# Transposes of a transformer block on the DMA crossbar instead of TensorE

## The chip, the cores and the metric

The kernel runs on one core of one Trainium2 chip. The metric is the device time of one execution in microseconds; lower is better. Before the change it is 750.04 us, the median of three runs (748.21 to 750.16).

## The reference

One layer on 2048 rows of width 1024, in bf16: a layernorm without scale or shift, sliding-window attention (32 heads of 32 columns, window of 256 rows, causal), a residual sum, a second layernorm, and a feed-forward part with SiLU (inner width 3584) and its own residual.

```python
def _layernorm(x, axis=-1, eps=1e-5):
    m = jnp.mean(x, axis=axis, keepdims=True)
    v = jnp.var(x, axis=axis, keepdims=True)
    return (x - m) / jnp.sqrt(v + eps)

def _A_ref(x, wqkv, wo):          # H = 32, Dh = 32, W = 256
    q, k, v = ...                 # x @ wqkv, split into heads
    scores = jnp.einsum("bhqd,bhkd->bhqk", q, k) * (Dh ** -0.5)
    mask = (idx[:, None] - idx[None, :] >= 0) & (idx[:, None] - idx[None, :] < W)
    p = _softmax(jnp.where(mask[None, None], scores, -1e9), axis=-1)
    return (p @ v, heads joined) @ wo

h  = x + _A_ref(_layernorm(x), A_wqkv, A_wo)
h2 = h + silu(_layernorm(h) @ B_w1) @ B_w2
```

(The attention function is abridged here: the split and joining of heads are written in words.)

## The kernel before

The 2048 rows are cut into four blocks of 512 rows (b = 0 to 3), each of four tiles of 128 rows (j = 0 to 3). TensorE multiplies along the partition axis, so whatever a product contracts over must lie on the 128 partitions. Three activations are produced with their rows on the partitions and are therefore transposed before use:

- the normalized input, tile by tile, into lnT_b (the helper ln_transpose, lines 173 to 176): eight 128x128 transposes on TensorE into the PSUM tile tp_ps, then one copy of 128x1024 out of it;
- the normalized attention result, by the same helper, into ln2T;
- the attention output of one group of four heads, from a ring of three SBUF tiles obuf into qT (attn_transpose, lines 281 to 285): four transposes into tp_ps, then one copy of 128x512. The result takes the place of the queries of that head group, which are no longer needed.

There is one tp_ps for all of them. The copies are VectorE's, but for block 0 of the first layernorm, whose copies are ScalarE's.

The program is written out in the order in which each engine is to work; there is no scheduler. Every engine and every DMA queue takes its instructions in that order and waits, instruction by instruction, for the data and the buffers that it needs. All transfers are issued on SP's queue.

The stages, in order:

1. Weights and the first rows are loaded. Block 0 is normalized and transposed tile by tile and its value projections follow (lines 293 to 300). Then come block 0's query and key projections in eight head groups (from line 327); with them, two steps after each group, run the statistics, normalization and transposes of block 1, as a list of small functions (ln1_steps).
2. Three attention loops, b = 1, 2, 3 (line 336 on). Loop b has 24 steps: 8 head groups of three score pieces, called A, B and C. In each step TensorE computes the scores of one piece for block b-1 into two PSUM tiles sc (a pair of heads in each), then one of the 24 projection products of block b (8 matmuls of 128x512), then one pending piece of the previous head group's end: attention output for the first pair of heads, for the second pair, and in the third step the transpose of that output. ScalarE takes the exponentials of the scores (two of them, one for each sc tile, line 242), GpSimd masks them. Loops 1 and 2 also carry the first layernorm of block b+1: its statistics and normalization from step 1 on, its four transposes at steps 11, 14, 17 and 20, each behind the attention transpose of that step. The loads of the next block's rows are issued at the head of a loop.
3. A last attention loop of 24 steps for block 3's scores. In place of the projections stand the output projections (wo_group) of blocks 0 to 2, each with a residual load, a sum on VectorE and, after every second, a store to h_dram. From step 9 on it carries the second layernorm of block 0 (ln2_steps): a load from h_dram, statistics, normalization, and the four transposes at steps 19 to 22. The feed-forward weights are loaded on the way.
4. Four feed-forward blocks (line 395 on). The first product of a block is 28 groups of 8 matmuls (h1_group, line 406), each followed by a tanh on ScalarE and a multiplication on VectorE. The end of the last head group (its attention transpose too) stands behind the first three groups of block 0, and block 3's output projections from group 6 on. The second product is 8 groups of 28 matmuls (line 448), two for each tile j; behind each group VectorE adds the residual (line 450) and SP stores 128 KB of the output (line 452). Two steps of the next block's second layernorm follow each group: load and first statistics behind group 1, and so on, the four transposes behind groups 6 and 7, two behind each.

The first product of a block needs all four transposed tiles before its first matmul, since one matmul takes 512 columns, those of the whole block. The same holds for the query and key products; a value product needs one tile alone.

Of the kernel before, what the change touches and what calls it, by code (L numbers as in the profile page):

```python
# [14 lines left out]
P = 128  # L15
# [21 lines left out]
def kernel(  # L37
# [10 lines left out]
    nc = tc.nc  # L48
# [36 lines left out]
    tp_ps = ps.tile([P, 1024], BF16, name="tp_ps")  # L85
    acc_ps = [ps.tile([P, 512], F32, name=f"acc{i}") for i in range(2)]

    def view(region, off, *dims):
        n = 1
        for d in dims:  # L90
            n *= d
        ap = region[:, off:off + n]
        if len(dims) == 2:
            return ap.rearrange("p (a b) -> p a b", b=dims[1])
        if len(dims) == 3:
            return ap.rearrange("p (a b c) -> p a b c", b=dims[1], c=dims[2])
        return ap
# [3 lines left out]
    lnT_b = [view(r_w, 24576, KT, 512), view(r_t, 0, KT, 512)]  # L101
# [4 lines left out]
    qT = [view(r_a, (4096, 8192, 12288, 0)[b], G, 512) for b in range(NB)]  # L106
# [7 lines left out]
    obuf = [view(r_n, 512 * i, 4, P) for i in range(3)]  # L114
    h_blk = [view(r_a, w2_off + 4096 * 4, 4, D)] + [view(r_e, 8192, 4, D)] * 3
    ln2T = [view(r_a, w2_off + 4096 * 5, KT, 512), view(r_e, 0, KT, 512), view(r_e, 4096, KT, 512), view(r_e, 0, KT, 512)]
# [22 lines left out]
    ident = const.tile([P, P], BF16, name="ident")  # L139
# [10 lines left out]
    def ln_stats(xt, st, j):  # L150
        stats = small.tile([P, 2, 6], F32, name="ln_st", tag="ln_st")
        for c in range(2):
            nc.vector.bn_stats(out=stats[:, c, :], in_=xt[:, c * 512:(c + 1) * 512])  # L153
        nc.vector.bn_aggr(out=st[:, j, :], in_=stats[:])

    def ln_rstd(st, rs, lo, hi):
        n = hi - lo
        var = small.tile([P, 4], F32, name="ln_var", tag="ln_var")
        t = small.tile([P, 4], F32, name="ln_t", tag="ln_t")
        va, ta, y = var[:, 0:n], t[:, 0:n], rs[:, lo:hi]  # L160
        nc.vector.tensor_scalar(out=va, in0=st[:, lo:hi, 1], scalar1=LN_EPS, scalar2=None, op0=ALU.add)
        nc.vector.tensor_scalar(out=y.bitcast(I32), in0=va.bitcast(I32), scalar1=1, scalar2=None, op0=ALU.logical_shift_right)
        nc.vector.tensor_scalar(out=y.bitcast(I32), in0=y.bitcast(I32), scalar1=-1, scalar2=0x5F3759DF, op0=ALU.mult, op1=ALU.add)
        for _ in range(3):
            nc.vector.scalar_tensor_tensor(out=ta, in0=y, scalar=-0.5, in1=va, op0=ALU.mult, op1=ALU.mult)
            nc.vector.tensor_tensor(out=ta, in0=ta, in1=y, op=ALU.mult)
            nc.vector.scalar_tensor_tensor(out=y, in0=ta, scalar=1.5, in1=y, op0=ALU.add, op1=ALU.mult)

    def ln_norm(xt, st, rs, j):
        nc.vector.tensor_scalar(out=xt, in0=xt, scalar1=st[:, j, 0:1], scalar2=rs[:, j:j + 1],  # L170
                                op0=ALU.subtract, op1=ALU.mult)

    def ln_transpose(xt, dst, j, copy):
        for kt in range(KT):
            nc.tensor.transpose(out=tp_ps[:, kt * P:(kt + 1) * P], in_=xt[:, kt * P:(kt + 1) * P], identity=ident[:])  # L175
        copy(out=dst[:, :, j * P:(j + 1) * P], in_=tp_ps[:].rearrange("p (k q) -> p k q", q=P))  # L176

    def ln_tiles(tag):
        st = small.tile([P, 4, 2], F32, name=f"st_{tag}", tag=f"st_{tag}")
        rs = small.tile([P, 4], F32, name=f"rs_{tag}", tag=f"rs_{tag}")  # L180
        return st, rs
# [98 lines left out]

    def attn_transpose(b, g):
        i = b * G + g
        for qt in range(4):
            nc.tensor.transpose(out=tp_ps[:, qt * P:(qt + 1) * P], in_=obuf[i % 3][:, qt, :], identity=ident[:])
        nc.vector.tensor_copy(out=qT[b][:, g, :], in_=tp_ps[:, 0:512])

    def tail_of(b, g):
        return [lambda: attn_out(b, g, 0), lambda: attn_out(b, g, 1), lambda: attn_transpose(b, g)]

    dve, act = nc.vector.tensor_copy, nc.scalar.copy  # L290
# [3 lines left out]
    for j in range(4):  # L294
        ln_stats(x_ring[j], st, j)
        ln_rstd(st, rs, j, j + 1)
        ln_norm(x_ring[j], st, rs, j)
        ln_transpose(x_ring[j], lnT_b[0], j, act)
        v_group(0, j, 0, act)
        v_group(0, j, 1, act)  # L300
# [3 lines left out]
    def ln1_steps(b):  # L304
        st, rs = ln_tiles("a")
        xs = [x_ring[(b % 2) * 4 + j] for j in range(4)]
        steps = [lambda j=j: ln_stats(xs[j], st, j) for j in range(4)]
        steps.append(lambda: ln_rstd(st, rs, 0, 4))
        for j in range(4):
            steps.append(lambda j=j: ln_norm(xs[j], st, rs, j))  # L310
        return steps, [lambda j=j: ln_transpose(xs[j], lnT_b[b % 2], j, dve) for j in range(4)]

    def ln2_steps(b):
        st, rs = ln_tiles("b")
        hb = h_blk[b]
        load = lambda: nc.sync.dma_start(out=hb, in_=h_dram[b * 512:(b + 1) * 512, :].rearrange("(j p) d -> p j d", p=P))
        steps = [load]
        steps += [lambda j=j: ln_stats(hb[:, j, :], st, j) for j in range(4)]
        steps.append(lambda: ln_rstd(st, rs, 0, 4))
        for j in range(4):  # L320
            steps.append(lambda j=j: ln_norm(hb[:, j, :], st, rs, j))
        for j in range(4):
            steps.append(lambda j=j: ln_transpose(hb[:, j, :], ln2T[b], j, dve))
        return steps

    steps = sum(ln1_steps(1), [])
    for g in range(G):
        qk_group(0, 0, g, act)
# [7 lines left out]
    for b in range(1, NB):  # L336
        dense = [lambda j=j, c=c: v_group(b, j, c, dve) for j in range(4) for c in range(2)]
        dense += [lambda w=w, g=g: qk_group(b, w, g, dve) for g in range(G) for w in range(2)]
        if b + 1 < NB:
            for j in range(4):  # L340
                load_x(b + 1, j)
            steps, turns = ln1_steps(b + 1)
        else:
            steps, turns = [], []
            nc.sync.dma_start(out=wo[:, 0:4, :], in_=wo_v[:, 0:4, :])
            nc.sync.dma_start(out=wo[:, 4:8, :], in_=wo_v[:, 4:8, :])
        n = 0
        for g in range(G):
            for kind in KINDS:
                scores(b - 1, g, kind)  # L350
                dense[n]()
                if pending:
                    pending.pop(0)()
                if steps and n >= 1 and n != 3:
                    steps.pop(0)()
                elif turns and n % 3 == 2:
                    turns.pop(0)()
                n += 1
            pending = tail_of(b - 1, g)
        assert not steps and not turns  # L360
# [8 lines left out]
    steps = []  # L369
    n = 0  # L370
    for g in range(G):
        for kind in KINDS:
            scores(NB - 1, g, kind)
            b, j, c = dense[n]
            if c == 0:
                nb, nj = (b, j + 1) if j < 3 else (b + 1, 0)
                if nb < NB - 1:
                    load_res(nb, nj, x2d)
            wo_group(b, j, c)
            if pending:  # L380
                pending.pop(0)()
            if n % 2 == 0 and n // 2 < KT:
                nc.sync.dma_start(out=w1[:, n // 2, :], in_=w1_v[:, n // 2, :])
            if n == 9:
                steps = ln2_steps(0)
            if n == 17:
                nc.sync.dma_start(out=w2[0], in_=w2_v[:, 0:4, :])
            if steps and n >= 9:
                steps.pop(0)()
            n += 1  # L390
        pending = tail_of(NB - 1, g)
# [28 lines left out]
    for b in range(NB):  # L420
# [4 lines left out]
        for ft in range(FT):  # L425
# [7 lines left out]
            if b == 0 and 6 <= ft < 14:  # L433
                j, c = divmod(ft - 6, 2)
# [4 lines left out]
        if b == 0:  # L439
            load_w2(6)  # L440
        steps = ln2_steps(b + 1) if b + 1 < NB else []
        for j in range(4):
            if j < 3:
                load_res(b, j + 1, h_dram)
            for c in range(2):
                acc = next_acc()
                for ft in range(FT):
# [5 lines left out]
                                  in_=t_out[j % 2][:, c * 512:(c + 1) * 512])  # L453
# [35 lines left out]
```

## Time and profile before

| | us |
|---|---|
| median of three runs | 750.04 |
| the profiled execution | 748.3 |
| its span, first to last instruction | 746.6 |
| TensorE matmuls busy | 708.6 |
| VectorE busy | 322.7 |
| ScalarE busy | 257.1 |
| copies out of tp_ps of 128x512, 32 on VectorE | 13.3 |

A profile is of one execution. Its span leaves out what lies before the first and behind the last instruction (1.7 us here). A row of the timeline gives the start in microseconds from the start of the span, the length, the engine (PE is TensorE's matmuls, PEld its weight loads, DVE VectorE, ACT ScalarE, POOL GpSimd, SPq the issuing of transfers on SP's queue), the line of the kernel, the operation, output and input, their shape, the count of instructions merged into the row, and in brackets how long the engine was idle before it and what ended that. Matmuls are pipelined: a row of several is shorter than their number times the length of one.

The DMA rows give a queue's packets, megabytes and the time that the packets took as a share of 16 engines; the rows of issues give the size of a transfer and the median time from issue to landing.

### The profile page before, as it was taken

How to read it: one execution, taken by the hardware profiler on the slowest of the kernel's cores; microseconds unless marked ns; L12 is line 12 of the kernel's file. 1: busy time of each engine (PE TensorE's matmuls, PEld its weight loads, DVE VectorE, ACT ScalarE, POOL GpSimd, SP SyncE). 2: the span in 40 equal slices, each digit the busy share in tenths (PEclk: the TensorE clock that was granted, in tenths of full speed). 3: DMA queues.
4: the chain of work that ended last, by engine and by line, in shares of the span. 5: the costliest groups of instructions: out<-in, count | busy, mean ns of one | idle time of the engine just before them, and what ended most of it. 6: DMA issues, size and time to landing. Idle time of an engine off the chain costs nothing.

```text
span 746.6 us, 12719 instructions
## 1 busy us (share of the span) xinstructions
PE 708.6 (95%) x5266; PEld 351.5 (47%) x5358; DVE 322.7 (43%) x705; ACT 257.1 (34%) x325; POOL 172.2 (23%) x375
## 2 busy tenths in 40 slices
PE   6899989988999999899999989999899999999997
PEld 3444545555555554454444444444444444444443
DVE  7356744854444445754343423325224343244111
ACT  2315555766777776642230003310023300133000
POOL 1004545665666766630000000000000000000000
PEclk9999999999999999999999999999999999999999
DMA  9510001000100177636204110012010021100010
GB/s 312 195 43 15 1 3 57 2 2 2 58 2 2 52 260 290 212 136 240 71 1 155 36 35 16 0 40 74 21 36 1 0 93 36 43 0 1 17 47 22
DMA packets 28138, 49.06 MB, mean 66 GB/s; under 512 B 1968, under 2 KB 12208, under 8 KB 28080
## 3 DMA queue, kind: packets, MB, share of 16 engines
q1 hardware_dynamic: 28080, 48.24, 19.1%
q8 instruction: 42, 0.69, 0.4%
q14 instruction: 16, 0.13, 0.1%
HBM read 39.85 MB, written 8.39 MB: 65 GB/s over the span
## 4 chain that ended last, share of the span: by engine, by line
PE 90%; DVE 5%; DMA 2%; issue 2%; ACT 1%; POOL 1%; DVEq 0%; ACTq 0%; POOLq 0%
PE hacc L406 17%; PE hacc L448 16%; PE acc L203 15%; PE acc L448 9%; PE acc L406 9%; PE acc L195 8%; PE o_ps L267 4%; PE acc L213 4%; PE sc L231 4%; PE tp_ps L175 2%; PE hacc L213 1%; DVE ln_st L153 1%; DMA r_a<-in_B_w_dram 1%; DMA r_a<-h_dram 1%; DVE r_t L450 1%
## 5 line engine op out<-in xcount | busy, mean ns | idle before, releaser
L242 ACT ACTIVATE r_e<-sc 128x1024 bf16<-128x1024 f32 (+2 forms) x192 | 175.8, 967 | 93.7 <-PE sc L231 89.9
L257 POOL TENSOR_SCALAR_AFFINE_SELECT r_e<-r_e 128x256 bf16<-128x256 bf16 (+1 forms) x368 | 169.2, 489 | 156.5 <-ACT r_e L242 153.3
L448 PEld LDWEIGHTS <-r_a 128*128 128x128 bf16 x896 | 87.4, 98 | 105.0 <-issue 0.8
L406 PEld LDWEIGHTS <-r_w 128*128 128x128 bf16 x896 | 87.4, 98 | 104.8
L448 PE MATMUL hacc<-r_a 128*128 128x512 bf16 x548 | 121.4, 379 | 0.6
L406 PE MATMUL hacc<-r_e,r_w 128*128 128x512 bf16 x452 | 100.7, 379 | 0.3
L415 ACT ACTIVATE r_n<-hacc 128x512 f32<-128x512 f32 x30 | 17.9, 597 | 191.5 <-PE hacc L406 190.4
L205 DVE CAST r_a<-acc 128x512 bf16<-128x512 f32 x56 | 38.6, 690 | 83.6 <-PE acc L203 83.6
L448 PE MATMUL acc<-r_a 128*128 128x512 bf16 x327 | 73.7, 379 | 1.0 <-DMA r_a<-in_B_w_dram 0.5
L203 PEld LDWEIGHTS <-r_w 128*128 128x128 bf16 x512 | 46.0, 98 | 57.9 <-issue 8.9
L203 PE MATMUL acc<-r_t,r_w 128*128 128x512 bf16 x240 | 57.7, 380 | 2.2 <-issue 2.1
L203 PE MATMUL acc<-r_w 128*128 128x512 bf16 x245 | 56.7, 380 | 1.4 <-issue 1.3
L267 PEld LDWEIGHTS <-r_e 128*128 128x128 bf16 x1440 | 45.6, 96 | 18.1 <-issue 3.2
L406 PE MATMUL acc<-r_e,r_w 128*128 128x512 bf16 x208 | 48.7, 379 | 0.4
L213 PE MATMUL acc<-r_o,r_a 128*128 128x512 bf16 x195 | 47.5, 380 | 1.6 <-issue 1.1
L267 PE MATMUL o_ps<-r_a,r_e 128*128 128x33 bf16 x1440 | 46.2, 178 | 2.6 <-DVE r_n L275 2.6
L450 DVE SCALAR_TENSOR_TENSOR r_t<-hacc,r_t 128x512 bf16<-128x512 f32 x20 | 13.7, 684 | 61.4 <-PE hacc L448 50.7
L231 PE MATMUL sc<-r_a 32*128 32x128 bf16 (+2 forms) x704 | 39.2, 275 | 0.0
L213 PEld LDWEIGHTS <-r_a 128*128 128x128 bf16 x256 | 23.1, 98 | 29.8 <-issue 5.2
L416 DVE SCALAR_TENSOR_TENSOR r_a<-r_n,hacc 128x512 bf16<-128x512 f32 x30 | 20.6, 688 | 33.0 <-ACT r_n L415 33.0
L450 DVE SCALAR_TENSOR_TENSOR r_t<-acc,r_t 128x512 bf16<-128x512 f32 x12 | 8.3, 691 | 59.7 <-PE acc L448 59.7
L195 PE MATMUL acc<-r_w 128*128 128x512 bf16 x122 | 29.0, 380 | 5.1 <-ACT r_w L176 4.5
(69 smaller groups left out, 514.5 us busy)
## 6 DMA issues: line engine op xcount, KB each, us to landing
r_w<-in_B_w_dram SPq DMA_DIRECT2D x8, 896.0 KB, 5.1
r_a<-in_B_w_dram SPq DMA_DIRECT2D x7, 1024.0 KB, 9.1
r_w<-in_A_wqkv_dram SPq DMA_DIRECT2D x6, 1024.0 KB, 11.2
r_o<-in_A_x_dram SPq DMA_DIRECT2D x16, 256.0 KB, 7.4
r_t<-in_A_x_dram SPq DMA_DIRECT2D x16, 256.0 KB, 3.5
h_dram<-r_t SPq DMA_DIRECT2D x16, 256.0 KB, 2.1
r_t<-h_dram SPq DMA_DIRECT2D x16, 256.0 KB, 2.7
out_dram<-r_t SPq DMA_DIRECT2D x32, 128.0 KB, 1.7
```

The source lines that it names most:

```text
L195: nc.tensor.matmul(acc, lhsT=lnT_b[b % 2][:, kt, j * P:(j + 1) * P], rhs=wqkv[:, kt, col0:col0 + 512], start=(kt == 0), stop=(kt == KT - 1))
L203: nc.tensor.matmul(acc, lhsT=wqkv[:, kt, col0:col0 + P], rhs=lnT_b[b % 2][:, kt, :], start=(kt == 0), stop=(kt == KT - 1))
L205: copy(out=(qT, kT)[which][b][:, g, :], in_=acc)
L213: nc.tensor.matmul(acc, lhsT=qT[b][:, g, j * P:(j + 1) * P], rhs=wo[:, g, c * 512:(c + 1) * 512], start=(g == 0), stop=(g == G - 1))
L231: nc.tensor.matmul(sc[hh // 2][:, hh % 2, ch * P:(ch + nq) * P], lhsT=kT[t // 4][r0:r0 + DH, g, (t % 4) * P:(t % 4 + 1) * P], rhs=qT[b][r0 ...
L242: nc.scalar.activation(out=e[:, :, lo:hi], in_=sc[pair][:, :, lo:hi], func=ACT.Exp, scale=scale)
L257: nc.gpsimd.affine_select(out=ap, in_=ap, pattern=[[0, 2], [0, n], [sgn, P]], compare_op=ALU.is_ge if upper else ALU.is_gt, fill=0.0, base ...
L267: nc.tensor.matmul(o_ps[:, qt * 2 + hh, 0:VW], lhsT=e_of(i, kind, pair)[:, hh, ch * P:(ch + 1) * P], rhs=v[:, b * 4 + kt, g * 4 + pair * 2 ...
L406: nc.tensor.matmul(acc, lhsT=w1[:, kt, ft * P:(ft + 1) * P], rhs=ln2T[b][:, kt, :], start=(kt == 0), stop=(kt == KT - 1))
L416: nc.vector.scalar_tensor_tensor(out=gT[:, ft, :], in0=th, scalar=1.0, in1=acc, op0=ALU.add, op1=ALU.mult)
L448: nc.tensor.matmul(acc, lhsT=gT[:, ft, j * P:(j + 1) * P], rhs=w2[ft // 4][:, ft % 4, c * 512:(c + 1) * 512], start=(ft == 0), stop=(ft == ...
L450: nc.vector.scalar_tensor_tensor(out=t_out[j % 2][:, c * 512:(c + 1) * 512], in0=acc, scalar=0.5, in1=t_in[j % 2][:, c * 512:(c + 1) * 512 ...
```

## The change

The four tiles of blocks 1 to 3 in the first layernorm, all sixteen tiles of the second, and the 32 attention outputs are transposed by a transfer from SBUF to SBUF through the crossbar, one per tile, on SP's queue. TensorE's transposes and the VectorE copies of these are gone. Block 0's four tiles of the first layernorm stay on TensorE. The places in the program's order are the same; what stood there in TensorE's and VectorE's order now stands there in SP's.

```diff
     def ln_transpose(xt, dst, j, copy):
+        if copy is None:
+            nc.sync.dma_start_transpose(out=dst[:, :, j * P:(j + 1) * P], in_=xt)
+            return
         for kt in range(KT):
             nc.tensor.transpose(out=tp_ps[:, kt * P:(kt + 1) * P], in_=xt[:, kt * P:(kt + 1) * P], identity=ident[:])
         copy(out=dst[:, :, j * P:(j + 1) * P], in_=tp_ps[:].rearrange("p (k q) -> p k q", q=P))
...
     def attn_transpose(b, g):
         i = b * G + g
-        for qt in range(4):
-            nc.tensor.transpose(out=tp_ps[:, qt * P:(qt + 1) * P], in_=obuf[i % 3][:, qt, :], identity=ident[:])
-        nc.vector.tensor_copy(out=qT[b][:, g, :], in_=tp_ps[:, 0:512])
+        nc.sync.dma_start_transpose(out=qT[b][:, g, :].rearrange("p (t q) -> p t q", q=P),
+                                    in_=obuf[i % 3].rearrange("p t d -> p (t d)"))
...
-        return steps, [lambda j=j: ln_transpose(xs[j], lnT_b[b % 2], j, dve) for j in range(4)]
+        return steps, [lambda j=j: ln_transpose(xs[j], lnT_b[b % 2], j, None) for j in range(4)]
...
-            steps.append(lambda j=j: ln_transpose(hb[:, j, :], ln2T[b], j, dve))
+            steps.append(lambda j=j: ln_transpose(hb[:, j, :], ln2T[b], j, None))
```

## The prediction

> **What bounds the kernel now.** I read the page's busy shares and its chain of waits first, then the windows of the three attention loops, then the timeline round each kind of transpose.
>
> ```profile
> PE 708.6 (95%) x5266; PEld 351.5 (47%) x5358; DVE 322.7 (43%) x705; ACT 257.1 (34%) x325; POOL 172.2 (23%) x375
> PE 90%; DVE 5%; DMA 2%; issue 2%; ACT 1%; POOL 1%; DVEq 0%; ACTq 0%; POOLq 0%
> 59.68:124.60 64.92, 59.90 (x624) 31.96 (x635) 38.58 (x91) 36.27 (x48) 34.36 (x78) 1.00 0.06 18
> 124.60:193.93 69.33, 64.09 (x810) 35.91 (x822) 40.45 (x97) 46.46 (x49) 44.67 (x97) 1.00 0.05 17
> 193.93:257.97 64.04, 62.57 (x790) 34.82 (x800) 27.79 (x65) 46.42 (x49) 44.38 (x97) 1.00 0.01 3
> ```
>
> TensorE sets the time: 95% busy and 90% of the chain, at a granted clock of 1.00 in the three windows. The last three rows are attention loops b = 1, 2, 3 (columns: length, then busy time of PE, PEld, DVE, ACT, POOL, clock, DMA share, GB/s). Loops 2 and 3 do the same work per step, but loop 2 also carries four layernorm transposes and is 69.33 - 64.04 = 5.29 us longer. DMA is nearly idle there (0.05 and 0.01), so the crossbar has room.
>
> A share of 95% doesn't say that every removed matmul is a gain, so I look at one plain head group of loop 3 (three score steps, kinds A, B, C), where only the attention transpose stands.
>
> ```profile
> 196.79 0.40 PE L231 MATMUL sc<-r_a 32*128 32x256 bf16 x8
> 199.56 0.40 PE L231 MATMUL sc<-r_a 32*128 32x128 bf16 x8
> 200.08 1.94 ACT L242 ACTIVATE r_e<-sc 128x1024 bf16<-128x1024 f32 x2 [0.83 <-PE sc L231]
> 201.63 0.39 PE L284 MATMUL tp_ps<-ident,r_n 128*128 128x128 bf16 x4
> 201.95 0.51 PE L231 MATMUL sc<-r_a 32*128 32x384 bf16 x8
> 202.54 1.94 ACT L242 ACTIVATE r_e<-sc 128x1024 bf16<-128x1024 f32 x2 [0.52 <-PE sc L231]
> 207.58 0.40 PE L231 MATMUL sc<-r_a 32*128 32x128 bf16 x8
> ```
>
> The two exponentials of C run from 200.08 to 202.02. The next scores (A) start at 201.95 and take 0.51 where the others take 0.40: their second pair of heads writes the score bank that the second exponential still reads. So the step C to A is already held by ScalarE, by about 0.11 us.
>
> **The change part by part.**
>
> *Attention transposes* (32 of four matmuls each).
>
> ```profile
> L284 PE MATMUL tp_ps<-ident,r_n 128*128 128x128 bf16 x128 | 12.4, 220 | 0.0
> ```
>
> One lasts 220 ns and four in a row 0.39, so the pitch is (0.39 - 0.22)/3 = 0.057 us and four cost TensorE 0.23. Thirty stand in C to A. Without them the first score matmuls start 0.23 us earlier and wait for the same exponential that ends at 202.02; the next exponential starts at 202.54 as before. I cost these thirty at **nothing**; if ScalarE had not bound, they would be worth 30 x 0.23 = 6.9 us. The last two, at the start of the feed-forward, have no scores behind them and give 2 x 0.23; one is counted in the second layernorm's part.
>
> *First layernorm, blocks 2 and 3* (eight transposes of 128x1024, always right behind an attention transpose).
>
> ```profile
> 182.15 0.40 PE L231 MATMUL sc<-r_a 32*128 32x128 bf16 x8
> 184.22 0.39 PE L284 MATMUL tp_ps<-ident,r_n 128*128 128x128 bf16 x4
> 185.49 0.61 PE L175 MATMUL tp_ps<-ident,r_o 128*128 128x128 bf16 x8 [0.89 <-DVE r_a L285]
> 186.03 0.40 PE L231 MATMUL sc<-r_a 32*128 32x384 bf16 x8
> ```
>
> C to A takes 186.03 - 182.15 = 3.88 here and 201.95 - 199.56 = 2.39 in the plain group: 1.49 more, of which 0.89 is the wait until VectorE has emptied the one PSUM tile that both kinds of transpose share. The step shrinks to the ScalarE bound, giving back the 0.11: 1.38. The loop windows give 5.29/4 = 1.32. I take 1.35: 8 x 1.35 = **10.8 us**.
>
> *First layernorm, block 1* (four, between query and key projections).
>
> ```profile
> 46.35 0.61 PE L175 MATMUL tp_ps<-ident,r_o 128*128 128x128 bf16 x8
> 46.80 3.62 PE L203 MATMUL acc<-r_w 128*128 128x512 bf16 x15
> 50.25 0.61 PE L175 MATMUL tp_ps<-ident,r_o 128*128 128x128 bf16 x8
> 52.23 3.62 PE L203 MATMUL acc<-r_w 128*128 128x512 bf16 x16
> 55.69 0.61 PE L175 MATMUL tp_ps<-ident,r_o 128*128 128x128 bf16 x8
> 56.13 3.62 PE L203 MATMUL acc<-r_w 128*128 128x512 bf16 x15
> ```
>
> Nothing else holds TensorE here: 0.45 + 1.98 + 0.44 = **2.9 us**. (50.25 starts two transposes, the second waiting for the copy of the first.)
>
> The trace makes eight transposes in a row last 0.61 us though one lasts 0.22: their pitch is 56 ns. The Trainium skill (TensorE: Matmul & The Clock Gate, Part 4: PE-mode transpose) gives some 275 ns for one in a kernel; priced so, the 352 removed would save 97 us and the time would be near 651. The rows above disagree, and I go by them.
>
> *Second layernorm, block 0* (steps 19 to 22 of the last attention loop).
>
> ```profile
> 312.25 0.40 PE L231 MATMUL sc<-r_a 32*128 32x256 bf16 x8
> 325.76 0.40 PE L231 MATMUL sc<-r_a 32*128 32x128 bf16 x8
> 328.05 1.89 PE L406 MATMUL acc<-r_a,r_w 128*128 128x512 bf16 x8
> ```
>
> B, C, A, B, C take 325.76 - 312.25 = 13.51; the same steps of the plain group take 207.58 - 196.79 = 10.79. Difference 2.7, plus 0.23 for the attention transpose before 328.05 and 0.23 for the one three groups later: **3.2 us**.
>
> *Second layernorm, blocks 1 to 3* (pairs behind groups 6 and 7 of the eight of the second feed-forward product).
>
> ```profile
> 428.79 0.69 DVE L450 SCALAR_TENSOR_TENSOR r_t<-acc,r_t 128x512 bf16<-128x512 f32 x1 [4.44 <-PE acc L448]
> 436.62 0.61 PE L175 MATMUL tp_ps<-ident,r_e 128*128 128x128 bf16 x8
> 436.82 0.69 DVE L450 SCALAR_TENSOR_TENSOR r_t<-acc,r_t 128x512 bf16<-128x512 f32 x1 [5.35 <-PE acc L448]
> 438.60 6.21 PE L448 MATMUL hacc<-r_a 128*128 128x512 bf16 x27
> 444.65 0.59 PE L406 MATMUL hacc<-r_e,r_w 128*128 128x512 bf16 x2
> ```
>
> A pair costs 438.60 - 436.62 = 1.98: two runs of eight and the wait for the first copy. Six pairs: **11.9 us**. The sum without new waits is 10.8 + 2.9 + 3.2 + 11.9 = **28.8 us**. VectorE loses 60 copies too, but it isn't on the path.
>
> **What the change adds** are 60 transfers on SP's queue, 28 of 256 KB and 32 of 128 KB, each behind everything SP was given earlier. The trace has no crossbar transfer; nearest are these rows of DMA.
>
> ```profile
> r_t<-h_dram SPq DMA_DIRECT2D x16, 256.0 KB, 2.7
> q1 hardware_dynamic: 4041, 4.55, 91.8%
> q1 hardware_dynamic: 919, 3.00, 78.5%
> q1 hardware_dynamic: 28080, 48.24, 19.1%
> 399.29 0.34 SPq L452 DMA_DIRECT2D out_dram<-r_t  x1
> ```
>
> The second row is the stretch 0 to 15 us, the third 290 to 300, the fourth the whole run. Time per packet on one engine: 15 x 16 x 0.918/4041 = 54.5 ns at 1.13 KB, and 10 x 16 x 0.785/919 = 137 ns at 3.26 KB. A line through both has 11 ns plus 38 ns per 1000 bytes. A block of 128x1024 cut into column runs of 256 bytes is 1024 packets, 64 per engine: 64 x 21 = 1.4 us (my estimate T of one transfer). The upper end: a packet costs 54.5 ns however small, T = 3.5; or the run's mean of 81 ns (0.191 x 16 x 746.6/28080), T = 5.2. The lower end is the plain transfer of 256 KB: 8 packets of 2 KB per engine at 89 ns, 0.7 us; the other 2.0 of its 2.7 us I take as fixed. I take T = 1.4, since both packet rows carry it.
>
> The place where this decides is the end of the second product. SP gets to the third and fourth transposes only behind the output store of group 7, whose VectorE instruction ends at 437.51; the store's issue takes 0.34. Group 8 starts at 436.62 in the new order and lasts 444.65 - 438.60 = 6.05, so the next block's first matmul wants all four at 442.67. They land at 437.85 + 2.0 + 2T = 442.65: just in time. The stall is 2T - 2.8 for each of the three blocks. Once the first two haven't landed either, counted from 428.79 + 0.69 + 0.34 = 429.82 to 428.59 + 2 x 6.05 = 440.69 (group 7 starts 0.2 before 428.79, as group 8 before 436.82), it is 4T - 8.9 (from T of 3). Block 0's place is as tight (its last store is one and a half steps ahead of 328.05); I treat it alike. For a margin of zero I allow 0.3 at each of four: 1.2 us.
>
> Elsewhere slack is large.
>
> ```profile
> 47.16 0.54 DVE L170 TENSOR_SCALAR r_o<-r_o,st_a,rs_a 128x1024 bf16<-128x1024 bf16 x1
> 15.26 41.39 SPq L125 DMA_DIRECT2D r_o<-in_A_x_dram  x12
> ```
>
> Block 1's rows are normalized by 47.70, 9 us ahead of their first use (loop 1 starts at 59.68 - 2.9). Loops 1 and 2 use theirs in the next loop. Attention outputs are read a loop later; their source ring has three places, so a transfer has two head groups (16 us) before VectorE wants the place again; behind the last one there are four groups of the feed-forward. On SP, the loads of block 3's rows, all issued by 56.65 before, now stand behind loop 1's transposes; their first statistics come one head group (8 us) behind the last of these, against 2.7 us for such a transfer. In the last loop each residual load comes at most one transposing transfer later, with two steps to spare. I cost these at nothing; a miss would hold VectorE, then TensorE, by a microsecond or two per place.
>
> Sum: 28.8 - 1.2 = 27.6. The profiled run took 748.3 (span 746.6), so 720.7; the median shown is 1.7 above it, from which 722.4. I forecast **722**.
>
> **The rivals.**
>
> *Slow crossbar, still a gain.* T = 3.5 by flat packets of 54.5 ns: 4 x (4 x 3.5 - 8.9) = 20 us of stalls, and 748.3 - 28.8 + 20 = 740 (rounded up). For it: fixed costs weigh most in small packets. Against: the two packet rows, which grow with bytes.
>
> *Slower than before.* The same mechanism at the same place decides the sign where 4 stalls eat 28.8, that is 4T - 8.9 = 7.2, T = 4.0. At the run's mean of 81 ns per packet T is 5.2, the stalls 4 x 11.9 = 48, the time 767. Serial blocks are its extreme: each 128x128 block one after another at the 1.7 us of the smallest store, T = 13.6, stalls of some 180 us, and about 900.
>
> ```profile
> out_dram<-r_t SPq DMA_DIRECT2D x32, 128.0 KB, 1.7
> ```
>
> The Trainium skill (VectorE: DVE Perf Modes, The three transpose paths) speaks this way: 1309 ns for a crossbar block against 390 for TensorE; eight in series would be an estimated 10.5 us and the time near 850. No run here shows it.
>
> *Attention transposes pay as well.* If the 0.11 us isn't ScalarE's, 6.9 more: 714. Against: the longer score group and the shortest ScalarE gap (0.52) stand together.
>
> *Nothing comes of it:* T near 4, gain and stalls cancel, 748.
>
> **How the numbers follow.** Forecast (T to about 2, 717 to 727) 0.62; slow but gaining (727 to 745) 0.16; attention transposes pay (712 to 716) 0.05; cancelled 0.03; slower 0.14, of which 0.05 serial blocks. Faster by over 0.3%, about what a measurement of this kernel can tell, is 0.83; within it 0.03; slower 0.14. The range from 714 to 743 leaves out the serial and slower cases and the ends of two others, some 0.2.
>
> **What would show it.** TensorE's transposes fall from 384 to block 0's 32. Loop 2 shrinks to loop 3's 64; loop 3 itself stays at 64, with the C to A gap of ScalarE still 0.52. The pairs vanish from the second product, and the next block's first matmul follows group 8 within half a microsecond. Transposes appear on SP with about 3.5 us to landing. Wrong would be TensorE waiting at line 406 on a transfer for several microseconds, or VectorE waiting at line 275 for the source ring.

## The result and the profile after

The changed kernel takes 720.5 us (median of four runs, 720.06 to 721.13) against 750.1 for the kernel before, run on the same chip: a ratio of 0.9607, 95% interval 0.9582 to 0.9631. The profiled execution took 720.06 us, with a span of 718.4, 28.2 less than before. The forecast was 722.

The busy shares of the changed kernel's page:

```profile
PE 695.8 (97%) x4920; PEld 330.1 (46%) x5006; DVE 294.2 (41%) x645; ACT 257.1 (36%) x325; POOL 172.9 (24%) x375
```

The windows of its attention loops 1 to 3 (length, busy time of PE, PEld, DVE, ACT, POOL, clock, DMA share, GB/s):

```profile
56.83:115.84 59.01, 57.78 (x564) 28.37 (x572) 33.85 (x80) 35.98 (x48) 33.96 (x77) 1.00 0.20 33
115.84:179.68 63.84, 62.74 (x745) 32.05 (x757) 35.06 (x84) 46.53 (x49) 45.08 (x97) 1.00 0.26 52
179.68:243.82 64.14, 63.04 (x757) 32.36 (x769) 25.24 (x56) 46.52 (x49) 44.64 (x97) 1.00 0.19 51
```

Loop 2, which carried the layernorm transposes, fell from 69.33 to 63.84; loop 3, where only the attention transposes went, is 64.14, as it was (64.04). Now the plain head group of loop 3 in the timeline (start, busy time, engine and line, instruction; what ended an idle time stands in brackets):

```profile
185.54 0.40 PE L234 MATMUL sc<-r_a 32*128 32x128 bf16 x8
...
186.06 1.94 ACT L245 ACTIVATE r_e<-sc 128x1024 bf16<-128x1024 f32 x2 [0.83 <-PE sc L234]
...
187.70 0.73 PE L234 MATMUL sc<-r_a 32*128 32x384 bf16 x8
...
188.52 1.94 ACT L245 ACTIVATE r_e<-sc 128x1024 bf16<-128x1024 f32 x2 [0.52 <-PE sc L234]
...
195.72 0.73 PE L234 MATMUL sc<-r_a 32*128 32x384 bf16 x8
```

The A scores start 0.22 us earlier, 2.16 behind the C scores where it was 2.39, and now last 0.73 instead of 0.51. The exponentials of C end at 186.06 + 1.94 = 188.00 and the next one starts 0.52 later, as before. The removed 0.23 us became a wait of the same length inside the scores, and the group is 195.72 - 187.70 = 8.02 us, unchanged.

The new transfers, first by the page's rows of DMA issues (median us from issue to landing last):

```profile
r_a<-r_n SPq DMA_TRANSPOSE x32, 2.4
r_e<-r_e SPq DMA_TRANSPOSE x12, 3.2
...
r_a<-r_a SPq DMA_TRANSPOSE x4, 3.9
```

The timeline at the end of the second feed-forward product, TensorE and SP:

```profile
418.70 6.21 PE L450 MATMUL hacc<-r_a 128*128 128x512 bf16 x28
...
420.00 2.61 SPq L175 DMA_TRANSPOSE r_e<-r_e  x2
...
424.74 1.24 PE L408 MATMUL hacc<-r_e,r_w 128*128 128x512 bf16 x5
```

The DMA view of the window 419.9 to 424.9 us, which holds two of them and one store:

```profile
q1 hardware_dynamic: 2256, 0.66, 64.2%
```

One transfer of 128x1024 holds SP for 2.61/2 = 1.30 us, and the packets of the window (the store's among them) take 5.0 x 16 x 0.642/2256 = 22.8 ns each on one of the 16 DMA engines. The next block's first matmul starts 424.74 - 418.70 = 6.04 us behind the start of group 8, the length of the group: no wait. One place does wait, the first product of block 0, in the timeline of SP and of TensorE:

```profile
306.67 1.08 SPq L221 DMA_DIRECT2D h_dram<-r_t  x1
...
307.81 2.71 SPq L175 DMA_TRANSPOSE r_a<-r_a  x2
...
312.44 1.89 PE L408 MATMUL acc<-r_a,r_w 128*128 128x512 bf16 x8 [1.02 <-DMA r_a<-r_a]
```

The store is of a residual sum that VectorE ends at 306.64, and SP gets to the last two transposes only behind it.

The span by stage. The boundaries of before are 328.05, which was shown, and these two of TensorE's timeline of before:

```profile
59.68 0.34 PE L231 MATMUL sc<-r_a 32*128 32x384 bf16 x4
...
258.06 0.51 PE L231 MATMUL sc<-r_a 32*128 32x384 bf16 x8
```

Those of after are 56.83, the start of loop 1's window, 312.44, and this row of TensorE's timeline:

```profile
243.82 0.73 PE L234 MATMUL sc<-r_a 32*128 32x384 bf16 x8
```

| stage | before | after | gain | forecast |
|---|---|---|---|---|
| up to attention loop 1 | 59.68 | 56.83 | 2.85 | 2.9 |
| attention loops 1 to 3 | 198.38 | 186.99 | 11.39 | 10.8 |
| last attention loop, to the first feed-forward matmul | 69.99 | 68.62 | 1.37 | 2.65 |
| feed-forward | 418.55 | 405.96 | 12.59 | 11.2 |
| span | 746.6 | 718.4 | 28.2 | 27.6 |

(The forecast column has the 0.3 us allowed for stalls taken off at its four places, and the last attention transpose counted with the feed-forward.)

### The profile page after: what moved, and what is told of

Same layout as the page of the kernel before. It is cut to its first block, busy times and chain, and to the rows that moved or that the text cites. A ratio compares the mean times of both kernels' runs of the same rounds, so it can differ in the third digit from the quotient of the medians.

```text
span 718.4 us, 12082 instructions
## 1 busy us (share of the span) xinstructions
PE 695.8 (97%) x4920; PEld 330.1 (46%) x5006; DVE 294.2 (41%) x645; ACT 257.1 (36%) x325; POOL 172.9 (24%) x375
## 4 chain that ended last, share of the span: by engine, by line
PE 91%; DMA 3%; DVE 2%; issue 1%; ACT 1%; POOL 1%; SPq 0%; DVEq 0%; POOLq 0%; ACTq 0%
PE hacc L408 18%; PE hacc L450 17%; PE acc L206 16%; PE acc L450 9%; PE acc L408 9%; PE acc L198 8%; PE sc L234 5%; PE o_ps L270 4%; PE acc L216 4%; PE hacc L216 1%; DMA r_w<-in_A_wqkv_dram 1%; DMA r_a<-h_dram 1%; DMA r_a<-in_B_w_dram 1%; DVE ln_st L153 1%; POOL r_e L260 1%
## 5 line engine op out<-in xcount | busy, mean ns | idle before, releaser
L206 PE MATMUL acc<-r_t,r_w 128*128 128x512 bf16 x242 | 58.5, 380 | 1.7 <-issue 1.4
L234 PE MATMUL sc<-r_a 32*128 32x128 bf16 (+2 forms) x704 | 46.9, 276 | 0.3
L452 DVE SCALAR_TENSOR_TENSOR r_t<-hacc,r_t 128x512 bf16<-128x512 f32 x20 | 13.7, 684 | 61.4 <-PE hacc L450 61.2
```

Of the source, the lines that this page charges most:

```text
L206: nc.tensor.matmul(acc, lhsT=wqkv[:, kt, col0:col0 + P], rhs=lnT_b[b % 2][:, kt, :], start=(kt == 0), stop=(kt == KT - 1))
L234: nc.tensor.matmul(sc[hh // 2][:, hh % 2, ch * P:(ch + nq) * P], lhsT=kT[t // 4][r0:r0 + DH, g, (t % 4) * P:(t % 4 + 1) * P], rhs=qT[b][r0 ...
L452: nc.vector.scalar_tensor_tensor(out=t_out[j % 2][:, c * 512:(c + 1) * 512], in0=acc, scalar=0.5, in1=t_in[j % 2][:, c * 512:(c + 1) * 512 ...
```

## The experiments

The theory: TensorE sets the pace except between score pieces C and A, where ScalarE does. So the gain is that of the layernorm transposes; the attention transposes stood in front of ScalarE's wait and give nothing; and the crossbar stays hidden because one matmul group covers it. The rivals: every transpose pays its own TensorE time; the longer A scores have another cause than ScalarE; the place of the transfers doesn't matter. All ratios are to the kernel before on the same chip.

### Half of the change at a time

The change with the attention transposes back on TensorE:

```diff
-        nc.sync.dma_start_transpose(out=qT[b][:, g, :]..., in_=obuf[i % 3]...)
+        for qt in range(4):
+            nc.tensor.transpose(out=tp_ps[:, qt * P:(qt + 1) * P], in_=obuf[i % 3][:, qt, :], identity=ident[:])
+        nc.vector.tensor_copy(out=qT[b][:, g, :], in_=tp_ps[:, 0:512])
```

> The changed kernel with the attention transposes put back on TensorE and VectorE; the 28 layernorm tiles stay on the crossbar. Theory (the attention transposes stand in front of a ScalarE wait, so they are worth nothing in the loops): about 721 us, at most 0.5 above the changed kernel's 720.5, with a head group of the third attention loop still 8.02 us long. Rival (every transpose pays its TensorE time, 32 x 0.23 us): 728 us and a head group of 8.25.

Measured: 721.9 us, ratio 0.9632 (0.9612 to 0.9653), 1.4 us over the changed kernel's median, where the theory allowed 0.5 and the rival wanted 7.5. The two intervals touch, and attention loops 1 to 3 took 245.82 - 58.49 = 187.33 us in the profiled execution against 186.99. The same group of loop 3, timeline of this kernel:

```profile
189.39 0.39 PE L287 MATMUL tp_ps<-ident,r_n 128*128 128x128 bf16 x4
189.71 0.51 PE L234 MATMUL sc<-r_a 32*128 32x384 bf16 x8
...
197.72 0.51 PE L234 MATMUL sc<-r_a 32*128 32x384 bf16 x8
```

The group is 197.72 - 189.71 = 8.01 us with the transposes and 8.02 without them.

The other half alone, the attention transposes on the crossbar and the layernorm ones on TensorE:

```diff
-        ... ln_transpose(xs[j], lnT_b[b % 2], j, None) ...
+        ... ln_transpose(xs[j], lnT_b[b % 2], j, dve) ...
-            steps.append(lambda j=j: ln_transpose(hb[:, j, :], ln2T[b], j, None))
+            steps.append(lambda j=j: ln_transpose(hb[:, j, :], ln2T[b], j, dve))
```

> The changed kernel with the layernorm transposes put back on TensorE and VectorE; the 32 attention transposes stay on the crossbar. Theory: the nine layernorm transposes that stood behind an attention transpose no longer wait 0.89 us for its copy and fill the ScalarE wait, so nine groups go from 9.40 to about 8.13; 9 x 1.27 + 0.46 = 11.9 us, so about 738 us, though the attention transposes alone are worth nothing beside the layernorm ones. Rival 1 (the two halves add up, attention 0): 750. Rival 2 (they add up and each pays its TensorE time): 743.

Measured: 739.5 us, ratio 0.9857 (0.9835 to 0.9879), the theory's 738 and neither rival's number. A group of loop 2 with a layernorm transpose:

```profile
168.97 0.40 PE L234 MATMUL sc<-r_a 32*128 32x384 bf16 x8
...
176.56 0.61 PE L178 MATMUL tp_ps<-ident,r_o 128*128 128x128 bf16 x8
177.10 0.40 PE L234 MATMUL sc<-r_a 32*128 32x384 bf16 x8
```

It lasts 177.10 - 168.97 = 8.13 us, with no wait left ahead of the transposes. Loops 1 to 3 took 248.91 - 61.05 = 187.86 us, 10.5 less than before. So the halves don't add: alone they save 28 and 11 us, together 30. What the attention half saves alone is the layernorm transposes' wait for its copy out of the shared PSUM tile, and the other half removes that wait too.

### ScalarE taken out of the way

Kind C's exponentials cut to half of their columns, with the crossbar transposes and with the attention transposes on TensorE:

```diff
+    for i in (4, 5, 10, 11):
+        nc.gpsimd.memset(ebuf[i], 1.0)
...
+        if kind == "C":
+            hi = 256
```

> The changed kernel, but the exponentials of kind C cover only the first half of the columns (the other half of these score tiles holds ones, so the output is not the layer's). Theory: ScalarE no longer holds the step from C to A, which goes from 2.46 to about 2.05 us; 31 x 0.4 = 12 to 13 us less, about 708. Rival (the longer A scores and the fixed step have another cause than ScalarE, e.g. the scores' own matmuls): 720.

> As the run with short C exponentials (half of kind C's columns left out), with the attention transposes on TensorE and VectorE. Theory: with ScalarE out of the way each attention transpose costs its 0.23 us, so this is 30 x 0.23 + 0.46 = 7.4 us slower than the short-C run with crossbar transposes, about 715. Rival (they cost nothing whatever bounds): the same as that run, within 1 us.

Measured: 713.4 us, ratio 0.9511 (0.9491 to 0.9531), and 720.2, ratio 0.9611 (0.9592 to 0.9630). The timeline of the kernel with crossbar transposes:

```profile
189.34 0.40 PE L236 MATMUL sc<-r_a 32*128 32x128 bf16 x8
...
191.50 0.40 PE L236 MATMUL sc<-r_a 32*128 32x384 bf16 x8
```

The timeline of the one with TensorE's:

```profile
191.82 0.40 PE L236 MATMUL sc<-r_a 32*128 32x128 bf16 x8
...
193.88 0.39 PE L291 MATMUL tp_ps<-ident,r_n 128*128 128x128 bf16 x4
194.20 0.40 PE L236 MATMUL sc<-r_a 32*128 32x384 bf16 x8
```

With a shorter exponential the A scores take 0.40 in both: their extra length was ScalarE's. C to A is 2.16 without and 2.38 with the transposes, and the two kernels differ by 6.8 us where 7.4 was expected. So the same edit is worth at most 1.4 us in front of ScalarE's wait and 6.8 without it. The first of them missed its own number by 5 us. TensorE's own step from C to A is 2.16, not 2.05; loops 1 to 3 gained 7.6 us (237.58 - 58.19 = 179.39 against 186.99), and the last attention loop nothing (306.18 - 237.58 = 68.60 against 68.62): a wait for VectorE grew there, as below.

### The cover of the transfers

The third and fourth transposes of blocks 1 to 3 moved behind the last group of the second product:

```diff
         for j in range(4):
+            if j == 2 and b > 0:
+                steps += [lambda: None, lambda: None]
             steps.append(lambda j=j: ln_transpose(hb[:, j, :], ln2T[b], j, None))
```

> The changed kernel with the third and fourth layernorm transposes of blocks 1 to 3 moved from behind group 7 of the second feed-forward product to behind group 8, so that no group covers them. Theory (that group is the cover, and two transfers take about 3.9 us from the first issue): they are issued 1.3 us after the last matmul and land 5.2 us after it; 3 x 5.2 = 15.6 us slower than the changed kernel, about 736, with a wait at line 408 of some 5 us in each block. Rival (transfers so short that their place doesn't matter): 721.

Measured: 745.9 us, ratio 0.9949 (0.9929 to 0.9969): the place matters, and the price was 25 us instead of 16. SP's transposes and the first matmul of the next block in this kernel's timeline:

```profile
427.72 2.62 SPq L175 DMA_TRANSPOSE r_e<-r_e  x2
...
432.23 2.29 PE L410 MATMUL hacc<-r_e,r_w 128*128 128x512 bf16 x5 [5.65 <-DMA r_e<-r_e]
```

Windows of this kernel (columns as above; the clock is the third number from the end):

```profile
432.00:434.00 2.00, 1.77 (x5) 0.69 (x6) 0.00 (x0) 0.00 (x0) 0.00 (x0) 0.50 0.70 229
434.00:436.00 2.00, 1.78 (x5) 0.63 (x5) 0.00 (x0) 0.16 (x1) 0.00 (x0) 0.50 0.00 0
...
438.00:440.00 2.00, 2.00 (x11) 0.94 (x10) 0.69 (x1) 0.87 (x2) 0.00 (x0) 1.00 0.00 0
```

The wait is 5.65 us, near the expected 5.2. But TensorE's granted clock falls to 0.50 in the idle time and stays there for the first ten matmuls: 5 in 2 us where later 10 or 11 fit, and still 5 when no transfer is under way (share 0.00). By windows of 1 and 2 us the clock is low for an estimated 4.2, 5.4 and 2.6 us of work in the three blocks, which loses half of that, some 6 us. With three waits (17 us) this is the price in the feed-forward, 743.5 - 314.08 = 429.42 us against 405.96. Most of what is missing to 25 was lost before 20 us in this execution (last section).

The first row of that timeline tells how close the cover is. The product starts 432.23 - 427.72 = 4.51 us behind the first issue; counted from 420.00 in the changed kernel, its transfers landed at about 424.5, an estimated 0.2 us before its product wants them.

To test the clock, 24 matmuls that nothing reads were put into each wait:

```diff
+        if b > 0:
+            for i in range(24):
+                nc.tensor.matmul(o_ps[:].rearrange("p a b -> p (a b)"), lhsT=w1[:, 0, 0:P], rhs=w1[:, 0, 0:512],
+                                 start=True, stop=True)
```

> The run with the last pair of transposes late (745.9, waits of 5.65 us, and 0.43 us instead of 0.21 for a matmul for about 4 us behind each), with 24 matmuls of 128x512 that nothing reads put into each wait (about 5.1 us). Theory (the idle TensorE lost its clock, 0.50 granted): the wait stays the same in length, the slow matmuls behind it go, 3 x 2.8 = 8.4 us less, about 737.5. Rival (the matmuls behind the wait are slow for another reason, such as the transfers still under way): 745.

Measured: 738.9 us, ratio 0.9854 (0.9835 to 0.9873), 7 us less though 72 matmuls more. The feed-forward took 736.8 - 313.58 = 423.22 us, 6.2 less, which is what the slow clock was estimated to cost. Its timeline:

```profile
425.73 5.34 PE L431 MATMUL o_ps<-r_w 128*128 128x512 bf16 x23
431.58 5.34 PE L410 MATMUL hacc<-r_e,r_w 128*128 128x512 bf16 x24 [0.50 <-issue]
```

A window of it:

```profile
432.00:434.00 2.00, 2.00 (x11) 0.92 (x10) 0.00 (x0) 0.49 (x1) 0.00 (x0) 1.00 0.49 188
```

The useful matmuls start 431.58 - 425.73 = 5.85 us behind the last group's end, so the wait is as long; the clock stays at 1.00, and with transfers still under way (share 0.49) the matmuls run at full rate. The rival that the transfers slow them falls.

### The last attention loop

Each second-layernorm transpose issued right behind its normalization:

```diff
-            steps.append(lambda j=j: ln_norm(hb[:, j, :], st, rs, j))
-        for j in range(4):
-            steps.append(lambda j=j: ln_transpose(hb[:, j, :], ln2T[b], j, None))
+            steps.append(lambda j=j: (ln_norm(hb[:, j, :], st, rs, j), ln_transpose(hb[:, j, :], ln2T[b], j, None)))
```

> The changed kernel with each second-layernorm transpose issued right behind its tile's normalization instead of behind all four. Theory (the 1.02 us wait before the first feed-forward product of block 0 is for the last two transposes, which stand on SP behind a store and an attention transpose): that wait is gone and the time is about 1 us less, 719.5; blocks 1 to 3, which did not wait, are unchanged. Rival (the wait has another last cause, such as the score banks that the feed-forward reuses): 720.5, with the wait still there.

Measured: 722.1 us, ratio 0.9626 (0.9608 to 0.9644): no gain. The profiled execution lost 1.5 us before loop 1 (last section), but the last attention loop, too, was longer, 314.67 - 245.36 = 69.31 us against 68.62. Rows of its timeline:

```profile
282.59 3.17 PE L216 MATMUL acc<-r_o,r_a 128*128 128x512 bf16 x7 [1.67 <-DVE r_t L218]
...
303.28 3.80 SPq L175 DMA_TRANSPOSE r_a<-r_a  x1
...
309.45 1.29 DVE L218 TENSOR_TENSOR r_t<-acc,r_t 128x512 bf16<-128x512 f32 x2 [5.49 <-DMA r_t<-in_A_x_dram]
...
310.19 1.89 PE L216 MATMUL acc<-r_o,r_a 128*128 128x512 bf16 x8 [1.34 <-DVE r_t L218]
...
314.67 1.67 PE L406 MATMUL acc<-r_a,r_w 128*128 128x512 bf16 x7
```

The wait at the first product is gone, so its cause was right. Another took its place: a transpose held SP for 3.80 us, the residual load behind it came late, VectorE waited 5.49 for it, and TensorE 1.34 for VectorE. The first row shows one cost more: behind a wait of 1.67 us a group of eight matmuls (one is missing from the trace) took 3.17 us where others take 1.90, at a granted clock of 0.50 from 284 to 286 us. Next, the same with the 1 MB weight load of step 17 moved to step 23:

```diff
-            if n == 17:
+            if n == 23:
                 nc.sync.dma_start(out=w2[0], in_=w2_v[:, 0:4, :])
```

> The run with each second-layernorm transpose behind its tile's normalization, where the wait at the first feed-forward product went away but VectorE then waited 5.49 us for a residual load that stood on SP behind a transpose of 3.80 us; here the 1 MB weight load of step 17 is also moved to step 23. Theory (that transpose was held up by the weight load ahead of it in the rings): no such wait is left, about 1 us under the changed kernel's 720.5, that is 719.5. Rival (the 1.2 to 1.3 us that SP spends on every transpose make the residual loads late by themselves): 722, with the VectorE wait still there.

Measured: 721.3 us, ratio 0.9614 (0.9593 to 0.9634): within the noise of the changed kernel, and neither number is told apart by the time. TensorE's timeline shows that wait gone and an older one longer:

```profile
282.25 0.59 PE L216 MATMUL acc<-r_o,r_a 128*128 128x512 bf16 x1 [3.11 <-DVE r_t L218]
```

In the changed kernel this wait was 0.88 us:

```profile
280.26 1.89 PE L216 MATMUL acc<-r_o,r_a 128*128 128x512 bf16 x7 [0.88 <-DVE r_t L218]
```

It comes from the second layernorm's statistics, which stand in VectorE's order ahead of a residual sum and wait for a 1 MB load. Why it lengthened when other loads moved was not tried by itself. Part of it needs no move: in the run with the filled waits, whose last attention loop is the changed kernel's own, the same wait was 2.38 us.

```profile
281.58 2.95 PE L216 MATMUL acc<-r_o,r_a 128*128 128x512 bf16 x7 [2.38 <-DVE r_t L218]
```

### A version that beats both

If ScalarE holds C to A and TensorE the other two steps, matmuls moved from these into that one should cost nothing. The projection groups were cut into single matmuls and dealt out 7, 7 and 10 to the steps A, B and C (the groups became generators, which is left out here; the last attention loop's output projections were dealt out in the same way):

```diff
+    SHIFT = (1, 0, 2)
+    def upto(groups, pos, n):
+        target = min(8 * (n + 1) + SHIFT[n % 3], 8 * len(groups))
+        while pos < target:
+            next(groups[pos // 8])
+            pos += 1
+        return pos
...
-                dense[n]()
+                pos = upto(dense, pos, n)
```

> The changed kernel with TensorE's work in the score steps evened out: the step of kind C takes the first two matmuls of the next projection group in addition to its own, that of kind A ends one matmul into the next. Nothing else moves. Theory (the step from C to A waits 0.33 us for ScalarE, the other two are TensorE's): 31 waits of 0.33 are filled, about 10 us less, 710.5, a head group of about 7.68 instead of 8.02 us. Rival (ScalarE's chain as a whole sets the 8.02): 720.5.

Measured: 715.3 us, ratio 0.9543 (0.9526 to 0.9559). Rows of TensorE's timeline in loop 3 and in the last loop:

```profile
183.51 0.40 PE L256 MATMUL sc<-r_a 32*128 32x384 bf16 x8
...
191.19 0.40 PE L256 MATMUL sc<-r_a 32*128 32x384 bf16 x8
...
273.14 0.38 PE L222 MATMUL acc<-r_o,r_a 128*128 128x512 bf16 x1 [3.02 <-DVE r_t L226]
...
305.84 1.89 PE L431 MATMUL acc<-r_a,r_w 128*128 128x512 bf16 x8 [1.25 <-DMA r_a<-r_a]
```

The group is 7.68 us, as expected, and the scores are back at 0.40. Loops 1 to 3 gained 6.8 us (236.84 - 56.69 = 180.15 against 186.99) of the 23 x 0.33 = 7.6 forecast there; the last loop gained nothing (305.84 - 236.84 = 69.00 against 68.62), with a wait for VectorE of 3.02 where it was 0.88. That faster score steps reach this wait sooner is likely but not shown, since it varied up to 2.38 without them. Three further versions moved transfers and statistics in that loop: both moves of the section above, then the 1 MB load one step earlier, then the statistics three steps later.

```diff
-            if n == 9:
+            if n == 8:
                 steps = ln2_steps(0)
+                steps[1:1] = [lambda: None] * 4
...
-            if steps and n >= 9:
+            if steps and n >= 8:
```

(The second of the three has one empty step here, and its statistics where they were.)

> The evened-out score steps (715.3) together with the two moves of the run before it (transposes behind the normalizations, weight load at step 23). Theory (the last attention loop, where the evened kernel gained nothing, is held by waits for transfers that share SP and the rings): about 1 us less than the evened kernel, 714. Rival: no change, 715.

> As the run before it, with the 1 MB load of block 0's rows for the second layernorm one step earlier (step 8) and its statistics where they were. Theory (VectorE's wait for that load, 3.6 us in the changed kernel, is what stops TensorE for 2 to 3 us in the last attention loop): about 2.5 us less, 711.5. Rival (the loop is held by the sum of its transfers, 253 GB/s): 714.

> As the evened kernel with all moves (713.4), with the first statistics of block 0's second layernorm three steps later (step 13 instead of 10), so that its 1 MB load, which took 8.1 us, has landed before VectorE comes to it. Theory (that wait of VectorE, 4.57 us there, stops TensorE for 3.1 us): the wait is gone and the time is about 3 us less, 710.5; the fourth transpose still stands at step 21. Rival (the loop is held by the sum of its transfers): 713.5, with the wait at another place.

Measured: 713.5 us, ratio 0.9513 (0.9496 to 0.9530); 713.4, ratio 0.9508 (0.9485 to 0.9532); and 709.9, ratio 0.9471 (0.9444 to 0.9497). The first is where its theory put it, but its interval touches that of the evened kernel, so its rival isn't ruled out. Judged by its time, the second missed: its load took 8.1 us (6.4 in the changed kernel), and VectorE still waited, by its timeline in that kernel:

```profile
272.78 1.29 DVE L153 BATCH_NORM_STATS2 ln_st<-r_a 128x6 f32<-128x512 bf16 x2 [4.57 <-DMA r_a<-h_dram]
```

The traces are kinder to the second. In the first of the three the load took 9.0 us and the last attention loop 306.38 - 236.70 = 69.68; here the loop is 305.84 - 238.54 = 67.30, the 2.4 less that was forecast, but this execution began loop 1 1.8 us later (58.39 against 56.55). One profile of each isn't proof.

With the statistics later, the last attention loop is 302.46 - 236.84 = 65.62 us against 68.62 in the changed kernel, by these rows of TensorE's timeline:

```profile
236.84 0.73 PE L256 MATMUL sc<-r_a 32*128 32x384 bf16 x8
...
302.46 1.90 PE L430 MATMUL acc<-r_a,r_w 128*128 128x512 bf16 x8 [0.69 <-DMA r_a<-r_a]
```

That version is 10.6 us faster than the change. TensorE is 98% busy in it. VectorE's wait did not go: it now waits 4.73 us for a residual load instead. But TensorE waits 1.86 us behind it, not 3.09, and its clock stays at 1.00. Of the 3.4 us between the profiled executions of the last two versions, 1.7 lie in this loop and 1.7 before loop 1.

## Why the prediction was right

- **TensorE sets the time, and the layernorm transposes are the gain.** Shown: without them on the crossbar 739.5, with them alone 721.9. The stages before the last attention loop gave 14.2 us where 13.7 was forecast, and the feed-forward's pairs vanished whole.
- **The attention transposes are worth nothing in the loops.** Shown from both sides: 8.01 and 8.02 us per group with and without them, once the layernorm transposes are gone; 6.8 us as soon as C's exponentials are cut; and the time returns when TensorE's work is moved into the wait. The reading rested on 0.11 us of one row, the A scores' 0.51 against 0.40, beside ScalarE's shortest gap.
- **The cost of a transfer.** T was estimated at 1.4 us from a line through two packet rows (21 ns for 256 bytes); the window gives 22.8 ns. The forecast had no price for SP itself, which each transfer holds for 1.30 us; that this is close to T is luck, since SP then feeds the transfers about as fast as their packets drain (64 x 22.8 ns = 1.46 us). It is the packet's price that kept the slower rival away: at a flat 81 ns the prediction's own sum has the change lose. Of the page that gives 1309 ns for a 128x128 block (the Trainium skill, VectorE: DVE Perf Modes, The three transpose paths) the trace says that it is no rate: eight blocks took SP 1.30 us, and landed in 3.2.
- **The place that decides.** The stall behind group 8 was forecast at zero with 0.3 us allowed, and was zero, with an estimated 0.2 us to spare. That the group was the cover is shown by the run without it. The formula for longer stalls was too kind, though: it priced idle time alone, and 5.65 us idle cost 23.46/3 = 7.8. By this the rival at 740 was priced too low.
- **The mis-sized term** is the second layernorm of block 0: 2.65 us forecast in its loop, 1.37 found. I treated its place like the other three, but on SP its last two transposes stand behind an attention transpose, a residual load and a store, and the first product waited 1.02 us for them. The other term is the price of a slot on SP: "at most one transposing transfer later" was costed at nothing. In this loop, where the DMA engines are 0.87 busy (0.63 before), a transpose mostly holds SP for 1.2 to 1.3 us, and a late load reaches TensorE through VectorE: the 1 MB load took 6.4 us where it was 5.6, VectorE waited 3.62 us for it where it was 2.9, and TensorE 0.88 for VectorE where it was 0.18. How much of that is SP's and how much the busier engines' stays open. Nor is the 1.37 a firm number: the same loop took 68.83 and 69.94 us in the runs with the last pair late and with the filled waits, 1.2 and 0.05 less than before. Zero stalls in the feed-forward and a little more in loops 1 to 3 made up for both terms; that the total came out 0.6 us from its forecast is luck to that extent.

## What to carry to other kernels

Before counting a removed matmul as a gain, look at what the next instruction of TensorE waits for: here, with the layernorm transposes gone, 30 of 32 identical edits were worth nothing, and a longer row of the same instruction was the clearest sign. Where such an edit frees an engine in front of another's wait, move work into the gap; that was worth 6.8 us in loops 1 to 3. A transfer that replaces an engine's work needs its cover named (the matmul group behind which it lands) and its slot on the issuing queue priced, above all where other loads share that queue.

## What the runs showed of the hardware

- A crossbar transpose held the issuing queue far longer than a plain store, and hardly by its size: 1.30 us for 128x1024 and 1.19 for 128x512, against 0.33. In the last attention loop, where the DMA engines are 0.87 busy, a plain store or load held it for up to 1.2 us, and one transpose for 3.80.

```profile
178.37 1.19 SPq L286 DMA_TRANSPOSE r_a<-r_n  x1
...
419.62 0.33 SPq L454 DMA_DIRECT2D out_dram<-r_t  x1
```

- TensorE lost half its clock in an idle time of 5.65 us, an estimated 3.0, 4.3 and 4.9 us after it began in the three blocks of the run with the last pair late, and had it back an estimated 4.2, 5.4 and 2.6 us after work resumed. The Trainium skill (TensorE: Matmul & The Clock Gate, Part 1: The HAM clock gate) has windows of about 3.4 us for both. The runs agree in size only. A wait of 1.67 us was enough in the run with each transpose behind its normalization, and 2.62 us in the one with short C exponentials left the clock at 1.00, as did waits of up to 1.42 in the changed kernel; so the length of one wait doesn't decide it here.
- Some executions lose a microsecond or two before 20 us, while the first loads are under way. The granted clock between 10 and 15 us was 0.66 to 0.72 in six of the 14 profiles and 1.00 in the other eight, and loop 1 began 58.2 to 58.5 us into the span in five of the six and 56.6 to 56.8 in the other kernels with block 1's rows on the crossbar. (In the sixth, with those rows on TensorE, it began at 61.05, against 59.68 before.) Why the clock falls there is open. It can be a part of any difference of a microsecond or two here. The window in the version with the earlier load:

```profile
10.00:15.00 5.00, 5.00 (x16) 1.90 (x15) 4.39 (x20) 0.59 (x1) 0.00 (x0) 0.66 1.08 356
```

The same in the changed kernel:

```profile
10.00:15.00 5.00, 3.97 (x24) 1.86 (x22) 4.39 (x20) 1.94 (x3) 0.00 (x0) 1.00 1.08 357
```
